# The opening written out up to slot 22, chunk 1 in the geometry of the later chunks, and eight-column softmax pieces on GpSimd

## The chip, the cores and the metric

The kernel runs on one core of a Trainium2 chip. Its time is the device time of one execution in microseconds; lower is better. A core has a matrix engine (TensorE, PE in the rows), a vector engine (VectorE, DVE), an activation engine (ScalarE, ACT), GpSimd (POOL) and a queue engine that issues most transfers (SyncE, SP). Each engine takes its instructions strictly in the order of its own program and waits on the others by semaphores.

## What is computed

Windowed attention over 8 batches, 8 heads, 576 tokens and 64 features per head (heads 0 to 3 with a plain window of 32 keys, heads 4 to 7 with a window of 32 keys at a step of 4), and behind it a feed-forward layer over the 4608 tokens with softplus between its two products (512 to 2048 to 512 features).

```
scores = (q @ k.T) / 8, masked to the window
attn   = exp(scores - max) / (sum(exp(scores - max)) + 1e-9)
x      = attn @ v                       # to [4608, 512]
h      = x @ w_in
out    = softplus(h) @ w_out
```

## The kernel before

The tokens are cut into 9 chunks of 512. A chunk's attention is done in 4 groups (pr 0 and 1 with the plain window, 2 and 3 with the stepped one), numbered `4 * chunk + pr`: groups 0 to 3 are chunk 0, 4 to 7 chunk 1, 8 to 11 chunk 2. The feed-forward work of the first three chunks is cut into 48 slots (`RUNS`): slots 0 to 4 are chunk 0 with the blocks 0 to 4 of 128 hidden features, 5 to 14 chunk 1 with blocks 0 to 9, 15 to 25 chunk 0 with blocks 5 to 15, then the rest of chunk 1 and chunk 2. A slot is four `h_part`s (x to hidden, three matmuls each, since every operand is a high and a low part), a softplus, and four `o_part`s (hidden to output, three matmuls each). The weights arrive as 64-bit words, and each of the 32 tiles (`ff`, 0 for w_in and 1 for w_out) is decoded on the chip: a pass on ScalarE, four on VectorE, a copy on ScalarE and a subtraction on VectorE. From slot 22 on, a planner in the program (costs, due times) writes out the order; the change does not touch it.

The order before slot 22 comes from two sources. `OPENING` is a string of words, each of which emits its instructions on the engines they belong to, in the order of the string; it goes up to the `h_part`s of slot 9 and the `o_part`s of slot 7. Behind it, up to slot 21, a loop emits `h_part`s and `o_part`s in turn, with softplus pieces, chunk 2's attention (`attend`, at the times `ATTENDED` and `VALUED`) and what is left of the decoding between them by a running account of VectorE's time. The words, by engine:

- SP: `k q v` load a group's keys, queries, values, `m` a mask, `r` a decoded tile's raw words (two halves of 256 KB each); the first 90 of these loads have at most 6 under way.
- PE: `F`/`f` fillers that read a zeroed tile and whose result nobody reads, `S` scores (64 small matmuls, and 2 that add the mask), `T` four transposes of the weights, `V` 64 small matmuls with the values, `H{slot}_{kt}` and `O{slot}_{m}` one part.
- DVE: `M` maximum (and, in a group of chunks 0 and 1, the scaling of the 8 columns `nm` by 1/8), `Z` divisor (guard of the 8 sums `sm`, then the reciprocal `ri`), `Pv` division of the 512 columns, `Xt` transposes of the result, `Xl` its low part, `G` softplus's last step, `Gl` its low part, `D1 D2 D3 D4` and `Dl` the decoding.
- ACT: `E` eight exponentials, `C` copy of the transposed weights, `Xh` high part of x, `A` abs, exp and log of a slot, `Gs` high part, `D0` and `D5` of the decoding, `K` copy of an output bank that is set aside.

A group runs S, M, E, Z, Pv, T, C, V, Xt, Xh, Xl. `H` of a slot needs `Xl` of the two groups that make its half of x (`H0_0` and `H0_1` groups 0 and 1, `H0_2` and `H0_3` groups 2 and 3), `Dl` of its w_in tile, and for its first part `G` of the slot two before. `O` needs `Gl` of its slot and `Dl` of its w_out tile. Groups of chunk 2 and later are laid out by heads instead (`self.c >= FIRST`): no division and no turn on PE; the weights are turned in squares on VectorE, sent to memory and fetched back, and the result is divided when it is read from PSUM, by eight copies with a scale on ScalarE (`shares`). `PLACES` says for each of the first 8 groups which PSUM banks its scores, its turn and its result use.

Of the kernel before, what the change touches and what calls it, by code (L numbers as in the profile page):

```python
# [109 lines left out]
D2_4_1 C6 O2_2 V6 D3_4_1 Z7 D2_3_1 D3_3_1 Xt6 D4_3_1 D0_5_0 G4 Pv7 O2_3 H6_0 D5_3_1 Xh6 Gs3 Xl6 D4_4_1  # L110
D1_5_0 r15 T7 r16 m2 r17 q8 r18 H6_1 Dl3_1 D2_5_0 Gl3 C7 Gs4 V7 r19 D0_7_0 D5_4_1 O3_0 O3_1 D1_7_0 Xt7
Dl4_1 Xh7 Xl7 Gl4 H5_2 H5_3 D0_6_1 O3_2 H6_2 H6_3 D1_6_1 D3_5_0 D2_6_1 A5 O3_3 O4_0 O4_1 D4_5_0 D5_5_0
G5 O4_2 H7_0 D2_7_0 A6 Dl5_0 D3_7_0 D3_6_1 K0 D0_6_0 Gs5 r20 G6 H7_1 O4_3 D1_6_0 D4_6_1 H7_2 H8_0 H8_1
H8_2 D4_7_0 Gl5 D5_6_1 r21 k8 v8 r22 Gs6 D5_7_0 K1 Dl6_1 D2_6_0 Dl7_0 r23 D0_8_0 K2 D0_5_1 K3 H8_3 H7_3
# [2049 lines left out]
```

## Time and profile before

| | |
|---|---|
| median of 3 runs | 830.92 us (830.21 to 831.73) |
| the profiled execution's own time | 832.8 us |
| its span, first to last instruction | 831.0 us |
| PE busy in the span | 804.5 us (97%) |
| DVE busy | 655.4 us (79%) |
| ACT busy | 607.6 us (73%) |
| POOL busy | 57.6 us (7%) |
| mean granted TensorE clock | 0.993 |

The median is what a change is compared with; the rows are of the profiled execution, which took 1.9 us more than the median. Busy time on PE is modelled at a matmul's end and overlaps the next one, so work is better read from the distance between starts. Source lines are those of the kernel before.

### The profile page before, as it was taken

The page shows a single profiled execution, that of the slowest core. Times are in us where ns is not written, and L with a number is a line of the kernel's source. Part 1 is how long each engine was busy: PE and PEld are TensorE (multiplying, and loading weights), DVE is VectorE, ACT ScalarE, POOL GpSimd, SP SyncE. Part 2 cuts the span into 40 slices and gives each one's busy share as a digit, 9 for nine tenths or more (in the row PEclk, how much of TensorE's full clock was granted, in tenths as well). Part 3 has the DMA queues.
Part 4 walks back from the last instruction along what each step waited for, and adds up shares of the span by engine and source line. Part 5 has one row for each costly group of instructions (what it writes and reads, how often), then busy time and mean ns, then how long its engine had stood idle before and what let it go on. Part 6 is the DMA issues. An engine that isn't in the chain of part 4 may idle for free. (4 is left out here: it accounts for less than half of the span.)

```text
span 831.0 us, 19932 instructions
## 1 busy us (share of the span) xinstructions
PE 804.5 (97%) x7861; PEld 648.8 (78%) x7861; DVE 655.4 (79%) x966; ACT 607.6 (73%) x1436; POOL 57.6 (7%) x70
## 2 busy tenths in 40 slices
PE   6789999999999999999999999999999999999997
PEld 3566887887888877778788888878878888888886
DVE  6788889887778779868779988777789877567964
ACT  6677789868787787698899836878887436776732
POOL 0000000030334423000000000000000000000000
PEclk9799999999999999999999999999999999999999
DMA  8973953455999989757787967988877576666662
GB/s 296 320 224 130 307 185 122 134 188 177 330 307 330 311 310 337 265 196 217 225 274 245 322 226 261 290 292 286 243 228 235 167 245 222 190 203 210 219 199 82
DMA packets 105806, 198.35 MB, mean 239 GB/s; under 512 B 9584, under 2 KB 52592, under 8 KB 105712
## 3 DMA queue, kind: packets, MB, share of 16 engines
q1 hardware_dynamic: 105568, 196.78, 71.9%
q8 instruction: 62, 1.02, 0.5%
q10 hardware_dynamic: 144, 0.29, 0.1%
q14 instruction: 32, 0.26, 0.1%
HBM read 148.80 MB, written 48.23 MB: 237 GB/s over the span
## 5 line engine op out<-in xcount | busy, mean ns | idle before, releaser
L246 PE MATMUL o_ps<-g,t 128*128 128x512 f32 x867 | 208.7, 389 | 0.0
L246 PEld LDWEIGHTS o_ps<-g,t 128*128 128x128 f32 x867 | 162.0, 188 | 33.9
L246 PE MATMUL o_ps<-g,parts 128*128 128x512 f32 x576 | 144.1, 393 | 2.1 <-ACT s L488 1.6
L246 PE MATMUL h_ps<-xh,parts 128*128 128x512 f32 x384 | 131.5, 400 | 5.0 <-DVE e L757 2.2
L246 PEld LDWEIGHTS o_ps<-g,parts 128*128 128x128 f32 x576 | 106.7, 188 | 26.7 <-ACT s L488 2.5
L1574 ACT CAST g<-stored 128x1024 fp32r<-128x1024 f32 x72 | 75.6, 1051 | 61.8 <-PE o_ps L246 58.2
L1578 DVE TENSOR_TENSOR g<-stored,g 128x1024 fp32r<-128x1024 f32 x72 | 87.8, 1220 | 27.5 <-ACT g L1574 27.3
L246 PEld LDWEIGHTS h_ps<-xh,parts 128*128 128x128 f32 x384 | 72.8, 190 | 23.6 <-ACT xh L676 3.1
L488 ACT ACTIVATE s<-s,nm 128x64 f32<-128x64 f32 x224 | 75.3, 355 | 4.7 <-DVE nm L477 3.8
L246 PE MATMUL h_ps<-xl,parts 128*128 128x512 f32 x192 | 75.9, 396 | 0.9 <-DVE xl L680 0.9
L894 POOL TENSOR_TENSOR a<-a 128x256 f32<-128x256 f32 x64 | 56.6, 892 | 258.6 <-DVE a L889 239.6
L246 PE MATMUL h_y<-s,t 128*128 128x512 f32 x276 | 70.6, 391 | 0.0
L246 PE MATMUL h_x<-s,t 128*128 128x512 f32 x276 | 70.5, 391 | 0.0
L246 PEld LDWEIGHTS h_x<-s,t 128*128 128x128 f32 x276 | 51.6, 188 | 11.1 <-issue 0.2
L246 PEld LDWEIGHTS h_y<-s,t 128*128 128x128 f32 x276 | 51.5, 188 | 11.0
L1554 DVE SCALAR_TENSOR_TENSOR stored<-stored,e 128x1024 f32<-128x1024 f32 x48 | 58.2, 1216 | 2.2 <-ACT e L1550 2.1
L1569 DVE TENSOR_TENSOR stored<-stored 128x1024 f32<-128x1024 f32 x48 | 58.1, 1214 | 0.2
L623 ACT ACTIVATE pt<-sv_ps,ri 128x64 f32<-128x64 f32 x224 | 48.7, 331 | 10.4 <-DVE s L465 7.7
L1544 ACT ACTIVATE e<-stored 128x1024 f32<-128x1024 f32 x48 | 50.6, 1056 | 3.0 <-DVE stored L1533 2.3
L1550 ACT ACTIVATE e<-e 128x1024 f32<-128x1024 f32 x48 | 50.7, 1060 | 1.0
L1547 ACT ACTIVATE e<-e 128x1024 f32<-128x1024 f32 x48 | 50.7, 1057 | 0.7
L757 DVE SCALAR_TENSOR_TENSOR e<-h_ps,e 128x512 f32<-128x512 f32 x48 | 32.8, 684 | 18.5 <-ACT e L1249 12.3
(107 smaller groups left out, 1250.2 us busy)
## 6 DMA issues: line engine op xcount, KB each, us to landing
t<-w_o SPq DMA_DIRECT2D x84, 512.0 KB, 4.3
raw<-w SPq DMA_DIRECT2D x64, 256.0 KB, 5.2
v<-vp SPq DMA_DIRECT2D x28, 512.0 KB, 5.5
t<-w SPq DMA_DIRECT2D x20, 512.0 KB, 4.1
t<-w_two SPq DMA_DIRECT2D x20, 512.0 KB, 4.6
q<-qp SPq DMA_DIRECT2D x35, 256.0 KB, 4.5
k<-kl SPq DMA_DIRECT2D x28, 320.0 KB, 4.7
w_o<-stage SPq DMA_DIRECT2D x32, 256.0 KB, 4.7
```

Of the source, the lines that this page charges most:

```text
L246: return tc.keep_in_program_order(nc.tensor.matmul(**kw))
L488: pin(nc.scalar.activation(out=self.blocks[:, t], in_=src, func=AF.Exp, bias=self.nm[:, t : t + 1], scale=1.0 / 8.0 if self.masked else 1. ...
L623: divided = nc.scalar.activation(out=self.x[:, n], in_=self.values_in[h][:, at_col : at_col + D], func=AF.Copy, scale=self.ri[:, n : n + 1],)
L757: pin(nc.vector.scalar_tensor_tensor(out=e, in0=tiles.pop(i), scalar=0.0, in1=e, op0=ALU.max, op1=ALU.add))
L894: pin(nc.gpsimd.tensor_tensor(out=out, in0=in0, in1=in1, op=ALU.subtract))
L1544: pin(nc.scalar.activation(out=es[key], in_=raw_g(*key), func=AF.Abs))
L1547: pin(nc.scalar.activation(out=es[key], in_=es[key], func=AF.Exp, scale=-1.0))
L1550: pin(nc.scalar.activation(out=es[key], in_=es[key], func=AF.Ln, bias=1.0))
L1554: pin(nc.vector.scalar_tensor_tensor(out=h, in0=h, scalar=0.0, in1=es.pop(key), op0=ALU.max, op1=ALU.add))
L1569: pin(nc.vector.tensor_tensor(out=raw_g(c, *PLACE[name]), in0=raw_g(c, *PLACE[a]), in1=raw_g(c, *PLACE[b]), op=op))
L1574: pin(nc.scalar.copy(out=set_of(k)[0], in_=raw_g(c, *PLACE[name])))
L1578: pin(nc.vector.tensor_tensor(out=low, in0=raw_g(c, *PLACE[name]), in1=high.bitcast(F32), op=ALU.subtract))
```

## The change

The string `OPENING` now goes up to the end of slot 21's `h_part`s and slot 19's `o_part`s, and the loop, `attend`, `tick`, `decoding` and the events are gone. The new words `U X Y W` are a chunk-2 group's turn, send, fetch and shares; `N` is the second maximum of such a group, and `K4` to `K7` the second set of output banks that is set aside. Thirteen large fillers become one (`F1_0`), behind the first `h_part`. Chunk 1 (groups 4 to 7) takes the layout by heads (`BY_HEAD = 1`) for its keys, queries, values and masks, with its turn still on PE; its `Pv` is gone and it has `W`, the eight scaled copies, in its place; its mask is added from 32 rows through a second constant, `spread`. The scaling of `nm` is taken out of `M` and becomes a word: `Np` runs it on GpSimd (groups 1 to 7), `N` on VectorE (group 0). The guard of `sm` can be taken out of `Z`: `Ep` runs it on GpSimd (all groups but group 0). `PLACES` changes. The instructions that the planner writes from slot 22 on are the same.

```diff
-OPENED = 9
-PLACES = "aoa hoa ooo aoa hoa oaa oaa aaa".split()
+PLACES = "hoa oaa oao aoa haa ooa oaa aaa".split()
+BY_HEAD = 1
-ATTENDED = 10.2, 12.9, 15.6, 19.0
-VALUED = 14.6, 17.1, 19.8
 OPENING = """
-F1 F6 f21 F4 r0 m0 F2 k0 q0 D0_0_0 r1 D0_1_0 D1_0_0 S0 k1 q1 D2_0_0 D3_0_0 D4_0_0 D5_0_0 M0 D1_1_0
-D2_1_0 S1 q3 k3 Dl0_0 E0 M1 D3_1_0 D4_1_0 k2 Z0 q2 S3 S2 k4 E1 M3 D5_1_0 q4 Pv0 T0 M2 E3 Z1 Pv1 Z3 r2 m1
-v0 S4 Dl1_0 M4 v1 C0 k5 q5 r3 E2 T1 V0 C1 D0_0_1 Pv3 Z2 Pv2 T2 Xt0 D1_0_1 Xh0 v2 Xl0 V1 E4 Xt1 Xh1 C2
-D2_0_1 Xl1 D3_0_1 D0_2_0 v3 r4 S5 M5 D4_0_1 Z4 H1_0 E5 r5 D1_2_0 D2_2_0 D3_2_0 k6 q6 H0_0 Pv4 T3 H1_1 r6
-v4 C3 D5_0_1 V2 Xt2 Xh2 T4 Z5 Xl2 C4 V3 r7 Xt3 Xh3 D4_2_0 k7 v5 Pv5 H0_1 D0_1_1 Xl3 D5_2_0 D1_1_1 H1_2
-H1_3 D0_3_0 Dl0_1 A1 Dl2_0 H0_2 H0_3 S6 D1_3_0 D2_3_0 A0 D3_3_0 T5 C5 G1 H2_0 D2_1_1 D3_1_1 D4_3_0
-D5_3_0 H2_1 G0 H2_2 H2_3 M6 Dl3_0 Gs1 Gs0 Gl0 V4 H3_0 H3_1 H3_2 D0_4_0 D0_2_1 D1_2_1 D2_2_1 Xt4 Xh4
-D4_1_1 Xl4 H3_3 O0_0 E6 Gl1 Z6 D5_1_1 D3_2_1 D4_2_1 Dl1_1 D1_4_0 D2_4_0 A2 O0_1 O0_2 G2 V5 Xt5 Xh5
...
-O7_1 r29 r30 Gs8 Dl8_0 Dl5_1 G9 O7_2 Gl8 Dl6_0 O7_3 Gs9 r31 Gl9
+q1 k1 m0 S1 M1 q0 k0 S0 M0 N0 r0 r1 D0_0_0 D1_0_0 D2_0_0 D3_0_0 f21 Np1 E1 Ep1 Z1 D0_1_0 D1_1_0 D2_1_0
+D3_1_0 q3 k3 S3 M3 E0 Pv1 q2 Np3 E3 Ep3 k2 S2 Z0 Pv0 T0 C0 q4 q5 m1 v0 k4 r2 r3 V0 D4_0_0 D5_0_0 M2 Np2 E2
+Ep2 D4_1_0 D5_1_0 Z3 Pv3 Xt0 Xh0 D0_0_1 Dl0_0 S4 M4 Dl1_0 D0_2_0 T1 C1 Z2 Pv2 D1_0_1 D2_0_1 Np4 E4 Ep4
+D1_2_0 Xl0 v1 V1 Xt1 Xh1 k5 D2_2_0 D3_2_0 S5 M5 Np5 Xl1 r4 v3 v2 r5 r6 q6 T2 D0_1_1 D3_0_1 D1_1_1 T3 C3 C2
+H0_0 D2_1_1 E5 Ep5 F1_0 D4_2_0 D5_2_0 V3 Xt3 Xh3 V2 Xt2 Xl3 D4_0_1 D0_3_0 Xh2 Xl2 D1_3_0 Z4 D0_2_1 D1_2_1 Z5
+T5 C5 H1_0 H0_1 T4 C4 D2_3_0 Dl2_0 D3_3_0 D4_3_0 D5_0_1 Dl0_1 H0_2 H0_3 A0 D3_1_1 G0 H1_1 H1_2 H1_3 A1 G1
+D2_2_1 D5_3_0 Dl3_0 r7 k6 v4 v5 r8 q7 r9 r10 r11 S6 M6 Np6 V4 W4 D0_4_0 Gs0 Gs1 Xt4 Xh4 D4_1_1 Xl4 Gl0
+D1_4_0 Gl1 D2_4_0 D3_2_1 D3_4_0 D4_4_0 D0_4_1 D5_1_1 Dl1_1 E6 Ep6 V5 W5 Xt5 H2_0 H2_1 H2_2 H3_0 H2_3 O0_0
+D1_4_1 O0_1 H3_1 H3_2 H3_3 k7 S7 r12 r13 r14 O1_0 O1_1 O0_2 O0_3 M7 Np7 A2 G2 D4_2_1 O1_2 O1_3 D5_4_0 Dl4_0
+A3 G3 Xh5 D2_4_1 Xl5 H4_0 H4_1 H4_2 H4_3 D3_4_1 D5_2_1 D0_3_1 Gs2 Gl2 D1_3_1 Dl2_1 O2_0 D2_3_1 D3_3_1 r15 E7
+D4_4_1 Z6 D0_5_0 T6 H5_0 H5_1 D1_5_0 D0_6_1 v6 C6 V6 Ep7 Z7 O2_1 D1_6_1 D2_6_1 D4_3_1 A4 W6 Gs3 O2_2 O2_3 k8
+v7 r16 r17 G4 D3_6_1 D4_6_1 Gl3 Xt6 T7 D0_5_1 D5_4_1 D1_5_1 D2_5_1 H6_0 H6_1 C7 V7 D5_3_1 Dl3_1 O3_0 O3_1
+O3_2 O3_3 Xh6 Xl6 Gs4 W7 Gl4 Dl4_1 O4_0 O4_1 Xt7 Xh7 D2_5_0 D5_6_1 D0_7_0 D0_6_0 Xl7 H5_2 D3_5_0 D1_7_0
+D3_5_1 D1_6_0 D4_5_1 D2_7_0 H5_3 A5 H6_2 H6_3 A6 m2 r18 q8 D4_5_0 D2_6_0 O4_2 r19 r20 K2 S8 G5 O4_3 G6
+D3_7_0 D4_7_0 D3_6_0 Dl6_1 H7_0 H7_1 H8_0 H8_1 H7_2 H8_2 H7_3 H8_3 Gs5 K3 Gl5 K0 O5_0 D5_7_0 D5_5_1 Dl5_1
+D4_6_0 Gs6 Gl6 O6_0 Dl7_0 D5_5_0 Dl5_0 k9 M8 K1 O5_1 O5_2 D5_6_0 A7 G7 D0_8_0 D1_8_0 N8 D0_7_1 D0_8_1 D1_7_1
+D2_7_1 O5_3 Gs7 Gl7 D1_8_1 D3_7_1 D0_9_0 D1_9_0 A8 G8 O6_1 O6_2 H9_0 H9_1 H9_2 O6_3 H9_3 A9 Gs8 O7_0 H10_0
+O7_1 O7_2 D2_9_0 D2_8_0 D3_8_0 D4_8_0 Dl6_0 D4_7_1 G9 D2_8_1 D3_8_1 E8 D5_7_1 O7_3 Gs9 H10_1 H10_2 Gl8 H11_0
+H11_1 H10_3 O8_0 H11_2 H11_3 D5_8_0 D4_8_1 D3_9_0 Gl9 Dl7_1 U8 A10 G10 Dl8_0 D4_9_0 A11 D0_10_0 q9 r21 r22
+S9 m3 r23 r24 r25 r26 r27 r28 D1_10_0 D2_10_0 Ep8 r29 D0_9_1 D1_9_1 D5_8_1 D5_9_0 Z8 G11 D2_9_1 Dl8_1 D3_9_1
+O8_1 O8_2 O8_3 Gs10 O9_0 O9_1 Gl10 D0_10_1 D1_10_1 M9 O9_2 O9_3 H12_0 H13_0 H12_1 H12_2 Gs11 Gl11 Dl9_0
+D3_10_0 q10 H12_3 D0_12_0 A12 O10_0 O11_0 O10_1 O10_2 D0_11_0 D4_10_0 D5_10_0 D4_9_1 D5_9_1 N9 G12 D2_10_1
+Dl10_0 O10_3 Gs12 Gl12 D3_10_1 D4_10_1 D1_12_0 D2_12_0 X8 Y8 k10 v8 V8 W8 Xt8 E9 U9 Dl9_1 D1_11_0 O11_1
+H13_1 H13_2 H13_3 A13 D2_11_0 G13 H14_0 D5_10_1 D3_12_0 D3_11_0 D4_12_0 Dl10_1 S10 O11_2 H14_1 H14_2 H14_3
+O11_3 D0_13_0 Gs13 Gl13 D0_11_1 A14 G14 X9 m4 M10 N10 H15_0 H15_1 O12_0 H15_2 H15_3 A15 O13_0 O12_1 O12_2
...
+O18_2 O18_3 H21_3 Ep11 Gs20 Gl20 A21 Dl15_1 Z11 X11 Y11 O19_0 O19_1 O19_2 O19_3
 """
-            self.n, self.scaled_by, self.beside = c * NPR + pr, None, None
-            self.own, self.masked = c == 0, c < 2
+            self.n, self.scaled_by, self.beside, self.guarded = c * NPR + pr, None, None, False
+            self.own, self.masked, self.by_head = c == 0, c < 2, c >= BY_HEAD
             self.places = PLACES[self.n] if self.n < len(PLACES) else "aaa"
 
-            if self.c >= FIRST:
-                src = kl[self.c - FIRST, self.pr]
+            if self.by_head:
+                src = kl[self.c - BY_HEAD, self.pr]
-                        col = t * WKEYS
-                        if self.c >= FIRST:
-                            q0, k0, col = g * PER + t * BLK, g * (PER + WIN) + t * BLK, col + t // 2 * MW
+                        if self.by_head:
+                            q0, k0 = g * PER + t * BLK, g * (PER + WIN) + t * BLK
+                        col = t * WKEYS + (t // 2 * MW if self.c >= FIRST else 0)
             if self.masked:
                 for r in range(2):
+                    if self.by_head:
+                        quad = slice(self.pr * SQ, (self.pr + 1) * SQ)
+                        matmul(
+                            out=self.banks[r][:, :SW], lhsT=spread[quad],
+                            rhs=masks[self.c][quad, r * SW : (r + 1) * SW], start=False, stop=True,
+                        )
+                        continue
-                pin(nc.vector.tensor_scalar(
-                    out=nm, in0=nm, scalar1=1.0 / 8.0, scalar2=1.0, op0=ALU.mult, op1=ALU.mult
-                ))
                 return
+        def smaller(self, engine):
+            if engine is nc.scalar:
+                pin(engine.activation(out=self.nm, in_=self.nm, func=AF.Copy, scale=1.0 / 8.0))
+                return
+            pin(engine.tensor_scalar(
+                out=self.nm, in0=self.nm, scalar1=1.0 / 8.0, scalar2=1.0, op0=ALU.mult, op1=ALU.mult
+            ))
+
         def greatest(self):
+            if self.masked:
+                self.smaller(nc.vector)
+                return
+        def guard(self, engine):
+            self.guarded = True
+            pin(engine.tensor_scalar(
+                out=self.sm, in0=self.sm, scalar1=1.0e-9, scalar2=1.0, op0=ALU.add, op1=ALU.mult
+            ))
+
         def divisor(self):
-            sm = self.sm
-            self.ri = ri = wk.tile([P, NB], F32, name="ri")
-            pin(nc.vector.tensor_scalar(
-                out=sm, in0=sm, scalar1=1.0e-9, scalar2=1.0, op0=ALU.add, op1=ALU.mult
-            ))
-            pin(nc.vector.reciprocal(out=ri, in_=sm))
+            self.ri = wk.tile([P, NB], F32, name="ri")
+            if not self.guarded:
+                self.guard(nc.vector)
+            pin(nc.vector.reciprocal(out=self.ri, in_=self.sm))
-            if self.c >= FIRST:
+            if self.by_head:
-            self.x = self.pt.rearrange("p g n -> p (g n)").rearrange("p (b n) -> p b n", n=D)
+            pt = self.pt.rearrange("p g n -> p (g n)") if self.c >= FIRST else self.pt
+            self.x = pt.rearrange("p (b n) -> p b n", n=D)
-            if self.c >= FIRST:
+            if self.by_head:
                 by_square = self.x.rearrange("p b (d k) -> p b d k", d=2)
-                x = x_half(self.c, self.dil)
+                x, j = x_half(self.c, self.dil) if self.c >= FIRST else None, self.j
+                if x is None:
+                    x, j = self.s.rearrange("p (d n) -> p d n", d=2), 0
+                    self.x = x
...
+    shared = {}
+
+    def score_of(n):
+        shared[n] = two_banks("sv_ps")
+        groups[n].score(shared[n])
+
+    def value_of(n):
+
+        m = partner(n)
+        if m < len(groups):
+            groups[n].weighted(shared.pop(m), groups[m])
+        else:
+            groups[n].weighted(two_banks("sv_ps"))
+
     parts = {
...
-        "F": fillers,
+        "F": lambda n, *_: fillers(n),
-        "m": load_mask,
+        "m": lambda n: load_mask(min(n, FIRST), max(n - FIRST, 0)),
-        "S": lambda g: groups[g].score(),
+        "S": lambda g: score_of(g) if g >= FIRST * NPR else groups[g].score(),
+        "N": lambda g: groups[g].greatest(),
+        "Na": lambda g: groups[g].smaller(nc.scalar),
+        "Np": lambda g: groups[g].smaller(nc.gpsimd),
+        "Ep": lambda g: groups[g].guard(nc.gpsimd),
...
-        "V": lambda g: groups[g].weighted(),
+        "V": lambda g: value_of(g) if g >= FIRST * NPR else groups[g].weighted(),
+        "U": lambda g: groups[g].turn_squares(),
+        "X": lambda g: groups[g].send_squares(),
+        "Y": lambda g: groups[g].fetch_squares(),
+        "W": lambda g: groups[g].shares(),
```

## Rows read from the trace of the kernel before

**Rows 1.** Us, busy PE, PEld, DVE, ACT, POOL, clock, DMA share, GB/s by stretch.

```profile
0.00:38.75 38.75, 26.56 (x719) 16.53 (x719) 25.68 (x64) 25.71 (x116) 1.02 (x6) 0.87 0.90 307
38.75:74.24 35.49, 31.61 (x497) 22.94 (x497) 30.17 (x62) 27.11 (x71) 0.00 (x0) 1.00 0.70 232
74.24:172.03 97.79, 97.10 (x842) 78.34 (x843) 85.83 (x163) 81.68 (x204) 0.00 (x0) 1.00 0.51 169
172.03:831.00 658.97, 649.28 (x5804) 531.03 (x5802) 513.76 (x680) 473.10 (x1047) 56.61 (x64) 1.00 0.75 245
```

**Rows 2.** VectorE's timeline: start us, duration us, line, operation.

```profile
38.06 0.69 DVE L680 TENSOR_TENSOR xl<-s,xh 128x512 fp32r<-128x512 f32 x1
...
73.55 0.69 DVE L769 TENSOR_TENSOR g<-e,g 128x512 fp32r<-128x512 f32 x1
```

**Rows 3.** TensorE's timeline.

```profile
73.38 0.73 PE L246 MATMUL o_ps<-g,parts 128*128 128x512 f32 x2
...
139.07 2.88 PE L246 MATMUL o_ps<-g,parts 128*128 128x512 f32 x12
...
172.03 0.39 PE L246 MATMUL h_ps<-xh,parts 128*128 128x512 f32 x1
```

**Rows 4.** VectorE's waits, 38.75 to 74.24: us in total, times, longest.

```profile
DVE sm L500 <- ACT s L488: 1.9, 1, 1.9
```

**Rows 5.** VectorE's timeline at 16 and at 86 us, back to back.

```profile
15.90 0.76 DVE L456 TENSOR_REDUCE nm<-s_ps 128x4 f32<-128x256 f32 x2
16.69 0.17 DVE L461 TENSOR_SCALAR nm<-nm 128x8 f32<-128x8 f32 x1
16.77 0.17 DVE L500 TENSOR_SCALAR sm<-sm 128x8 f32<-128x8 f32 x1
16.97 0.20 DVE L503 RECIPROCAL ri<-sm 128x8 f32<-128x8 f32 x1
17.20 0.69 DVE L506 TENSOR_TENSOR s<-s,ri 128x512 f32<-128x512 f32 x1
...
86.25 0.42 DVE L220 TENSOR_SCALAR a<-a 128x512 int32<-128x512 int32 x1
86.58 0.68 DVE L240 TENSOR_TENSOR parts<-a,parts 128x512 fp32r<-128x512 f32 x1
87.19 0.68 DVE L225 SCALAR_TENSOR_TENSOR a<-raw,a 128x512 int32<-128x512 int32 x1
```

**Rows 6.** ScalarE's timeline.

```profile
8.78 0.66 ACT L214 ACTIVATE a<-raw 128x512 f32<-128x512 f32 x1 [2.52 <-DMA raw<-w]
9.34 0.61 ACT L237 CAST parts<-a 128x512 fp32r<-128x512 f32 x1
9.85 0.32 ACT L488 ACTIVATE s<-s_ps,nm 128x64 f32<-128x64 f32 x1
...
12.51 0.31 ACT L488 ACTIVATE s<-s_ps,nm 128x64 f32<-128x64 f32 x1 [0.18 <-DVE nm L461]
...
78.15 0.60 ACT L750 ACTIVATE e<-h_ps 128x512 f32<-128x512 f32 x1 [1.74 <-PE h_ps L246]
...
129.39 1.73 ACT L623 ACTIVATE pt<-sv_ps,ri 128x64 f32<-128x64 f32 x8
```

**Rows 7.** DMA from 0 to 30 us.

```profile
DMA packets 4810, 8.87 MB, mean 296 GB/s; under 512 B 528, under 2 KB 784, under 8 KB 4805
```

**Rows 8.** Columns of rows 1, for one microsecond.

```profile
24.00:25.00 1.00, 0.00 (x0) 0.00 (x0) 0.14 (x1) 1.00 (x9) 0.00 (x0) 0.50 1.00 361
```

**Rows 9.** GpSimd's groups: count, busy us, mean ns, idle before.

```profile
L894 POOL TENSOR_TENSOR a<-a 128x256 f32<-128x256 f32 x64 | 56.6, 892 | 258.6 <-DVE a L889 239.6 <-DVE parts L916 13.3 <-DVE sm L500 3.2
...
L297 POOL CAST ident<-consts 128x128 f32<-128x128 bf16 x1 | 0.3, 290 | 4.7 <-DMA consts<-cst 4.7
```

**Rows 10.** VectorE's groups, 200 to 300 us, where GpSimd works.

```profile
L889 DVE TENSOR_TENSOR a<-parts 128x512 f32<-128x512 f32 x22 | 16.2, 757 | 0.0
...
L769 DVE TENSOR_TENSOR g<-e,g 128x512 fp32r<-128x512 f32 x16 | 10.9, 682 | 4.9 <-ACT g L763 4.6
```

More of the change, by code (lines that the diff above doesn't have):

```diff
@@ L110 @@
[L110 to L114, printed above, removed]
@@ L709, in values @@
         load_v(n + 1)
-    events, serial = [], itertools.count()
-    def at(when, part, *what, cost=0.0):
-        heapq.heappush(events, (when, next(serial), cost, part, what))
-    def send(n):
-        groups[n].send_squares()
-    def bring(n):
-        groups[n].fetch_squares()
-    def pump(now):
-        spent = 0.0
-        while events and events[0][0] <= now:
-            _, _, cost, part, what = heapq.heappop(events)
-            part(*what)
-            spent += cost
-        return spent
-    STEPS = 2 * NKT
     tiles, ready = {}, {}
@@ L800, in o_part @@
         if final and i < HANDED:
[L801 to L806 removed]
+            keeping[m] = c, o_ps[m]
     def kept_part(m, c, src):
@@ L814, in resumed_part @@
         load_dma(out=out[m * P : (m + 1) * P, c * CH : (c + 1) * CH], in_=obs[m])
-    def softplus_tile(i):
-        activated(i)
-        if i < HANDED - 1:
-            at(i + 1.0, softplus, i, cost=0.69)
-            at(i + 1.125, g_high, i)
-            at(i + 1.375, g_low, i, cost=0.69)
     def fillers(n):
@@ L866, in tile_windowed_attention_softplus_ffn @@
         name = word[:3] if word[0] == "D" and word[1] != "l" else word.rstrip("0123456789_")
-        parts[name](*(int(x) for x in word[len(name) :].split("_")))
+        parts[name](*map(int, word[len(name) :].split("_")))
     fetch(len(needed))
@@ L1066, in decoding @@
-    def decoding(keys):
-        def part(*steps):
-            for key, step in steps:
-                if key < len(keys):
-                    decode_step(*keys[key], step)
-        parts = []
-        for j in range(len(keys) + 1):
-            if j < len(keys):
-                begun = [(0, 0), (1, 0)] if j == 0 else []
-                parts.append((0.84, (*begun, (j, 1), (j, 2))))
-                parts.append((0.69, ((j, 3),)))
-            if j:
-                parts.append((0.69, ((j - 1, 6),)))
-            if j < len(keys):
-                parts.append((0.69, ((j, 4), (j, 5), (j + 2, 0))))
-        return [(0, cost, lambda what=what: part(*what)) for cost, what in parts]
@@ L1086, in tile_windowed_attention_softplus_ffn @@
-    chores = decoding([(ff, i) for _, ff, i in needed if (ff, i) not in words])
-    for j, (when, valued) in enumerate(itertools.zip_longest(ATTENDED, VALUED)):
-        attend(FIRST * NPR + j, when, valued)
-    behind = 0.0
-    def tick(time):
-        nonlocal behind
-        now[0] = time
-        behind += pump(time) - 0.69
-        while chores and behind + chores[0][1] < 0.4:
-            _, cost, chore = chores.pop(0)
-            chore()
-            behind += cost
-        behind = max(behind, 0.0)
@@ L1103, in tile_windowed_attention_softplus_ffn @@
-    for i in range(OPENED + 1, HANDED):
-        for kt in range(NKT):
-            h_part(i, kt)
-            if kt == NKT - 1:
-                softplus_tile(i)
-            tick(i + (kt + 1) / STEPS)
-        for m in range(NKT):
-            o_part(i - LAG, m)
-            tick(i + (NKT + m + 1) / STEPS)
-    pump(HANDED + 0.4)
-    for _, _, chore in chores:
-        chore()
-    assert not events
     MM, LATENCY, RATE, LANDING = 0.227, 0.06, 0.32, 2.3
@@ L2099, in _layout @@
     ], axis=1)
-    qp[FIRST:] = ql[FIRST:].reshape(qp[FIRST:].shape)
-    kl = np.empty((NCH - FIRST, 2, 2, 2, D, 4, per + WIN), np.float32)
-    late = np.empty((NCH - FIRST, 2, 2, 2, WKEYS, 2, 2, 4, D), np.float32)
-    for c in range(FIRST, NCH):
+    qp[BY_HEAD:] = ql[BY_HEAD:].reshape(qp[BY_HEAD:].shape)
+    kl = np.empty((NCH - BY_HEAD, 2, 2, 2, D, 4, per + WIN), np.float32)
+    late = np.empty((NCH - BY_HEAD, 2, 2, 2, WKEYS, 2, 2, 4, D), np.float32)
+    for c in range(BY_HEAD, NCH):
         for j in range(2):
@@ L2140 @@
     masks = _masks()
-    arrays["msk"] = _late_masks(masks).astype(ml_dtypes.bfloat16)
+    late = _late_masks(masks)[FIRST - BY_HEAD :]
+    arrays["msk"] = late.reshape(NCH - FIRST, NPR, P, 2 * SW).astype(ml_dtypes.bfloat16)
     eye = np.eye(P, dtype=ml_dtypes.bfloat16)
     arrays["cst"] = np.stack(
-        [np.concatenate([eye, (8.0 * m).astype(ml_dtypes.bfloat16)], axis=1) for m in masks[:2]]
+        [
+            np.concatenate([eye, np.tile(eye[:BLK, :BLK], (NG, NG)), (8.0 * m).astype(ml_dtypes.bfloat16)], axis=1)
+            for m in (masks[0], _late_masks(masks)[0, :, 0].reshape(P, 2 * SW))
+        ]
     )
```

100 lines of the change are left out of this document (30 added, 70 removed).

## The prediction, made before the change had run

> **What bounds the kernel now.** I read first the busy times cut at three points of the program [rows 1]: the end of the last low part of chunk 0's x (`Xl3`, the VectorE row that starts at 38.06 and takes 0.69), the end of what slot 3's first output part needs (`Gl3`, starting at 73.55) [rows 2], and the first `h_part` of slot 22, at 172.03 [rows 3]. The reader is to see two regimes. From 74 us on TensorE has 97.10 of 97.79 us busy, and after 172 us 649.28 of 658.97: there only less TensorE work would save time. Ahead of 74 us TensorE has gaps (31.61 of 35.49, and 26.56 of 38.75, fillers included), and VectorE is nearly full. Then I read what VectorE waits for between 38.75 and 74.24 [rows 4]: the largest wait, 1.9, is for a group's exponentials, that is, for the group's own chain.
>
> **The accounts.** The words of either string say how many passes each engine has ahead of a point, and the distance from start to start what a pass costs. VectorE [rows 5]: a maximum 0.79, the scaling of `nm` 0.08, the guard 0.20, the reciprocal 0.23, a 512-column pass 0.61, one that reads a single float tile (`D1`, `D2`) 0.33; an `Xt` I put at a long pass, 0.68. ScalarE [rows 6]: `D0` 0.56, a copy or cast 0.51, a group's eight exponentials 2.5 (the next group's start, less its 0.18 of idle), a slot's abs, exp and log 1.8 (three of 0.60), the eight scaled copies of a `W` 1.73.
>
> **TensorE's work** is the same in both: ahead of `O3_0` either list has 24 parts of `H`, 12 of `O` and 8 each of `S`, `T` and `V`, only in another order. From there to slot 22 the same matmuls remain. So the question is when `O3_0` can begin, and whether TensorE stays full behind it.
>
> **Stage 1, to the end of chunk 0's x.** VectorE before: 6 maxima, 6 scalings, 8 short and 10 long passes of the decoding, 6 whole `Z` (0.43), 6 `Pv`, 4 `Xt`, 4 `Xl`: 25.1 us, in 38.75, so 13.6 us are start and waiting. After, ahead of `Xl2`: 6 maxima, 1 scaling, 10 short and 10 long passes, one whole `Z` and three bare reciprocals, 4 `Pv` (chunk 1's two are gone), 4 `Xt`, 4 `Xl`: 22.8 us. With the same 13.6 of waiting it ends at 36.4; with 0.2 more for each of five GpSimd hops on the way, at 37.4, the upper bound. The lower bound is the loads. Up to `v2`, the last one needed, the new list loads 8,320 KB, 8.52 million bytes, and the first 30 us of before moved 8.87 million [rows 7], so `v2` lands about 28.8; `V2`, `Xt2`, `Xh2`, `Xl2` take some 0.9, 0.7, 0.6 and 0.7 behind it: 31.7. Between the two I walked the three lists with these costs: scores of group 1 at about 7, its exponentials from 9.5 (behind `D0_0_0`, whose raw words stand as far down the list, 1.8 million bytes, as those of the pass that began at 8.78 did before [rows 6]), E0 to 14.8, E3 to 17.5, E2 to 21, C1 to 23.7, V1 to 24.9, E4 to 26.0, Xl1 to 28.1, E5 to 30.6, V2 to 31.9, Xl2 to 34.4. I take 35.2, 0.8 more for what such a walk leaves out.
>
> The fillers cost nothing to remove where TensorE waits for loads, but they were also work on it. In before the clock stood at its upper level up to 23 us, and in the microsecond at 24, without a matmul in it, at 0.50 (1.2 of 2.4 GHz) [rows 8]. After the change the small blocks of `S`, `T` and `V` probably run at 1.2 GHz from the start; the walk costs them so.
>
> **Stage 2, from there to `O3_0`.** VectorE before: 14 short and 19 long passes of the decoding, 9 of softplus, 2 maxima with scalings, 2 whole `Z`, 2 `Pv`, 3 `Xt`, 3 `Xl`: 29.2 us, in 35.49, 6.3 over. ScalarE before: 7 `D0`, 15 copies, 5 slots, 2 groups' exponentials: 25.6. After, VectorE: 15 short, 21 long, 9 of softplus, 2 maxima, 4 bare reciprocals, 3 `Xt`, 2 `Xl`: 28.8. ScalarE: 7 `D0`, 17 copies, 5 slots, 2 exponentials and three `W`: 3.9 + 8.7 + 9.0 + 5.0 + 5.2 = 31.8. So the `W`s, which replace four divisions of 0.61 on VectorE by four times 1.73 on ScalarE, make ScalarE the longer one. Lower bound 31.8, upper 31.8 + 6.3 = 38.1. I take 34.2, under half of that surplus, because the wait of before [rows 4] sits in the chain E, Z, Pv, T, and in chunk 1 `T` now follows E directly.
>
> **Stage 3, from `O3_0` to slot 22.** The same matmuls: 97.8 (97.1 with the 0.7 of idle gone). VectorE has 85.83 busy there and ScalarE 81.68 [rows 1]; either keeps some 12 us of cover, which is what hides the rest of the edits: `K`, `W`, `U` and `Xt` of chunk 2 are the ones that the loop issued, and the raw loads end later (`r31` beside slot 14) but are asked for in the order of use. On SP `k10` and `v8` now stand behind `X8 Y8`, a trip to memory and back, and `V8` is the next word on TensorE that needs them: the first place where a wait could show.
>
> **The sum.** 35.2 + 34.2 + 97.8 = 167.2 instead of 172.0: 4.8 less. What follows slot 22 is the planner's list, untouched: 659.0. The span of 831.0 becomes 826.2, the execution's own 832.8 becomes 828.0, and, as that execution lies 1.9 above the median of the runs shown, the median 830.92 becomes 826.1. Bounds together: 31.7 + 31.8 + 97.1 = 160.6, 11.4 less; 37.4 + 38.1 + 97.8 = 173.3, 1.3 more.
>
> **GpSimd's pieces.** The trace has no pass of 8 columns on GpSimd. Its nearest rows are a cast of 128 columns, 0.29, and a two-input pass of 256 columns, 0.89 [rows 9]. VectorE's own was 0.08 from start to start, so a piece in the chain M, Np, E costs between 0.2 and 0.8 more. I take 0.3, near the cast; the walk has it. Behind an `Np` on ScalarE the whole list waits, copies and decoding too. `Ep` is covered: the `Z` behind it stands after other VectorE words. What speaks against: beside GpSimd's passes a two-input VectorE pass takes 0.757, away from them 0.682 [rows 10]. The Trainium skill (SBUF — State Buffer, Who interferes with whom) says that VectorE instructions with two SBUF inputs and GpSimd instructions that read SBUF lock each other out for a whole instruction. The two rows agree in direction only. By that rule, as an estimate, each of seven pieces could wait for one VectorE pass, and the sum would come near 831.
>
> **The rivals.**
> *More is gained*: stage 1 near its bound of loads and stage 2 near ScalarE's sum, 33 + 32 + 97.5 = 162.5, 9.5 less: 821.4. For it: both lists leave much room. Against: no stage ahead of 74 us has come near its sum before [rows 1].
> *ScalarE eats it*: stage 2 keeps 6.3 on top of ScalarE's 31.8, and stage 1 its 13.6: 36.4 + 38.1 + 97.8 = 172.3, no change, 831.2.
> *The written order starves TensorE later* (the slower side): where the order was a written string, in stage 2, TensorE stood 3.9 of 35.5 us, 11%; in stage 3, most of it written by the loop, 0.7 of 97.8. The stretch that is newly written, from slot 10 on, is some 72 us. At 11% it costs 7.9, and the kernel is slower by 3.1: 834.0. It decides from 4.8 us, 7%, on. Against it: the 12 us that VectorE and ScalarE have to spare there.
> *GpSimd holds the chain*: at 0.8 more for each of the seven `Np`, 5.6, against 2.1 in my sum: 3.5 later, 829.6; if each waits for a VectorE pass of 0.68 too, 4.8 more: 834.4.
> *The clock*: TensorE stays at 1.2 GHz until the `H` parts of slots 0 and 1 are done. Twelve matmuls in a row take 2.88 at the upper level [rows 3], 0.23 each; eight parts of three at double that are 5.5 us later, of which the ScalarE work beside them hides over half: 2.3 later, 828.4.
>
> **How the numbers follow.** A measurement tells 0.2%, 1.7 us, from no change. My forecast (823 to 829) has 0.45, more gained 0.14, the clock 0.08, ScalarE 0.11, the written order 0.13, GpSimd 0.09. Faster: 0.45 + 0.14 + 0.08 + 0.02 of the last two = 0.69; no change: 0.11 + 0.05 of these two = 0.16; slower: the other 0.15 of them. The time is that of the forecast, 826.1. The range is 821.0 to 832.5: it leaves out the very end of the gain and the slower ends of the last two.
>
> **What would show it.** Right: chunk 0's x complete near 35 instead of 38.75, `O3_0` near 69 instead of 73.4, slot 22 near 167, ScalarE busier than VectorE between the first two, and the same 659 behind slot 22. Wrong: TensorE idle by several us between 75 and 167; exponentials that wait for GpSimd; a half clock beyond 40 us; or another distance from slot 22 to the end.

## The result, and the profile after

The changed kernel takes 822.87 us (median of 4 runs, 822.52 to 823.02), the kernel before 831.33 beside it (830.21 to 831.97): a ratio of 0.990, interval 0.988 to 0.992, 8.4 us less. The prediction said 826.1, 4.8 less than the median it was made against. The profiled execution took 822.52 with a span of 820.7; that of before 832.8 and 831.0, so between the two traces there are 10.3 us to place.

The busy times after, by stretch (columns as in [rows 1]), cut at the end of chunk 0's x, at the first matmul of `O3_0` and at slot 22:

```profile
0.00:35.06 35.06, 22.85 (x708) 16.76 (x708) 23.14 (x53) 26.02 (x117) 4.40 (x16) 0.76 0.90 303
35.06:68.73 33.67, 31.37 (x496) 24.43 (x495) 28.49 (x59) 30.96 (x94) 1.17 (x4) 0.95 0.93 310
68.73:166.25 97.52, 97.52 (x850) 78.71 (x845) 87.56 (x164) 84.55 (x215) 1.55 (x4) 1.00 0.48 153
166.25:820.70 654.45, 648.32 (x5804) 530.72 (x5802) 508.90 (x672) 473.24 (x1044) 56.82 (x64) 1.00 0.76 248
```

The cuts come from these rows of the timelines after: VectorE, where `Xl2` is now the last low part of chunk 0's x [rows 2], and TensorE [rows 3].

```profile
34.37 0.69 DVE L718 TENSOR_TENSOR xl<-s,xh 128x512 fp32r<-128x512 f32 x1
```

```profile
68.73 4.62 PE L261 MATMUL o_ps<-g,parts 128*128 128x512 f32 x18
...
166.25 0.39 PE L261 MATMUL h_ps<-xh,parts 128*128 128x512 f32 x1
```

The marks lie at 38.75, 73.38 and 172.03 before [rows 1, 3] (the second stretch of [rows 1] ends 0.9 later, at 74.24). So 5.8 us are gained ahead of slot 22 (3.7 to the first mark, 1.0 to the second, 1.1 to the third), and 4.5 behind it, where the instructions are the same. From 68.73 to slot 22 TensorE has not one gap.

The stretch from 35 to 68.7 has one wait on TensorE (line of the waits; then its timeline, and ScalarE's `W4`):

```profile
PE a_ps L261 <- ACT pt L658: 2.3, 1, 2.3
```

```profile
42.75 1.35 PE L261 MATMUL a_ps<-v,pt 64*32 64x64 f32 x64 [2.28 <-ACT pt L658]
```

```profile
40.96 1.74 ACT L658 ACTIVATE pt<-a_ps,ri 128x64 f32<-128x64 f32 x8
```

It is `V5`, which writes the bank that `W4` reads, and `W4` stands behind two slots' softplus passes on ScalarE.

Behind slot 22, TensorE's waits before:

```profile
PE sv_ps L246 <- issue: 1.4, 1, 1.4
PE h_ps L246 <- DVE e L757: 1.2, 1, 1.2
PE h_y L246 <- issue: 1.0, 1, 1.0
PE h_x L246 <- DVE e L757: 0.8, 1, 0.8
PE sv_ps L246 <- PE h_y L246: 0.5, 1, 0.5
PE sv_ps L246 <- DMA pt<-turned: 0.4, 1, 0.4
...
```

and after:

```profile
PE h_ps L261 <- DVE e L773: 1.1, 1, 1.1
PE h_x L261 <- DVE e L773: 0.8, 1, 0.8
...
```

Two stops in which the profile shows nothing to wait for ("issue", 1.4 and 1.0, at 557 and 401 us) and a late fetch of turned weights near 607 (0.4 and 0.5) are gone: 3.3 us. Matmul for matmul, the distance between the two traces grows by 0.4 near 188 us, 1.1 at 401, 1.6 at 557 and 1.2 near 607, so 3.9 of the 4.5 lie at these three places. The 0.4 is a leftover of the order ahead of slot 22: a weight load of the kernel before waits for a low part.

```profile
188.07 1.00 PEld L246 LDWEIGHTS o_ps<-g,parts 128*128 128x128 f32 x5 [0.51 <-DVE g L769]
```

What makes the stops, the first four experiments ask.

### The profile page after: what moved, and what is told of

Read it like the earlier page. It is cut to its first block, busy times and chain, and to the rows that moved or that the text cites. A ratio compares the mean times of both kernels' runs of the same rounds, so it can differ in the third digit from the quotient of the medians.

```text
span 820.7 us, 19960 instructions
## 1 busy us (share of the span) xinstructions
PE 800.1 (97%) x7849; PEld 650.6 (79%) x7849; DVE 648.1 (79%) x945; ACT 614.8 (75%) x1468; POOL 63.9 (8%) x88
## 4 chain that ended last, share of the span: by engine, by line
PE 94%; ACT 2%; DVE 2%; DMA 0%; issue 0%; POOL 0%; SPq 0%; DVEq 0%; ACTq 0%; POOLq 0%
PE o_ps L261 44%; PE h_ps L261 16%; PE h_y L261 14%; PE h_x L261 14%; PE sv_ps L261 5%; ACT s L518 1%; PE s_ps L261 1%; PE a_ps L261 1%; DMA k<-kpl 0%; PE t_ps L551 0%; DVE a L381 0%; ACT pt L658 0%; DVE s L381 0%; ACT pt L589 0%; DVE nm L478 0%
## 5 line engine op out<-in xcount | busy, mean ns | idle before, releaser
L1502 DVE TENSOR_TENSOR g<-stored,g 128x1024 fp32r<-128x1024 f32 x72 | 87.8, 1221 | 26.1 <-ACT g L1498 25.9
L773 DVE SCALAR_TENSOR_TENSOR e<-h_ps,e 128x512 f32<-128x512 f32 x48 | 32.9, 686 | 23.0 <-ACT e L1173 17.3
```

The source lines that it names most:

```text
L773: pin(nc.vector.scalar_tensor_tensor(out=e, in0=tiles.pop(i), scalar=0.0, in1=e, op0=ALU.max, op1=ALU.add))
L1502: pin(nc.vector.tensor_tensor(out=low, in0=raw_g(c, *PLACE[name]), in1=high.bitcast(F32), op=ALU.subtract))
```

## The experiments

All ratios are to the kernel before, on the same chip, with 95% intervals. A time at slot 22 or behind it is that of one profiled execution.

**What is gained behind slot 22.** Both kernels once more, and the fillers taken out of the one and put into the other:

```diff
-F1 F6 f21 F4 r0 m0 F2 k0 q0 D0_0_0 ...
+r0 m0 k0 q0 D0_0_0 ...
```

```diff
-q1 k1 m0 S1 M1 q0 ...
+F1 F6 f21 F4 F2 q1 k1 m0 S1 M1 q0 ...
```

> The kernel before, unchanged, profiled a second time. In its first profile TensorE stood 1.0, 1.4 and about 1.1 us behind slot 22 (at 402, 557 and 611 us) and 4.8 us ahead of 27 us with nothing that the profile shows to wait for. Theory P (the place in the program makes these stops): the same stops at the same places, and again about 659 us from slot 22 to the end. Theory R (each execution has its own): stops elsewhere or none, slot 22 within 2 us of 172, and 655 to 658 us behind it.

> The changed kernel, unchanged, profiled a second time and timed beside the others. Theory P (the stops of TensorE behind slot 22 hang on where its instructions lie): slot 22 begins within 1 us of 166.25 and again about 654.5 us follow it. Theory R (each execution has its own stops): another distance, 654 to 659.

> The kernel before without its fillers (34 matmuls that nobody reads), everything else alike. In both its profiles it stopped behind slot 22 at the same places (at 401, 557 and 611 us, 3.1 and 3.7 us together). Theory P (these stops hang on where the instructions of TensorE lie, and any other count of them ahead moves them): other stops or none there, and up to 3.7 us less behind slot 22. Theory Q (they hang on the transfers of that time, which the fillers do not touch): the same stops. For the opening: theory A (the fillers hold the clock up): slot 22 begins 1 to 4 us later than 172; theory B (they only cover a wait for loads): at 171 to 173.

> The changed kernel with the first fillers of the kernel before (34 matmuls that nobody reads) back at the head of the list. Theory P (stops behind slot 22 hang on the number of instructions ahead of them on TensorE): stops there again, more than 655.5 us behind slot 22, and the time 1 to 3 us up by these alone. Theory Q (they hang on the transfers of that time): 654 to 655 again. In the opening, theory A (the fillers delay the scores or hold the clock): slot 22 moved by over 1 us; theory B (ScalarE's exponentials set the pace there): 165.5 to 167.

The kernel before again: slot 22 at 171.60 and 658.36 behind it, with stops of 1.2 and 0.7 at the two places of the first profile, as theory P has it. The changed kernel again: ratio 0.991 (0.989 to 0.993), slot 22 at 167.17, 655.23 behind it, no such stop, but 0.4 for the late fetch, which therefore comes and goes by the execution. Two executions of one kernel differ by 0.4 and 0.9 at slot 22, and by 0.6 and 0.8 behind it. Before without fillers: 0.998 (0.997 to 0.999), slot 22 at 171.05 (theory B) and 656.59 behind it; the two old places are free, and one stop, of 0.6, stands at 592. So a change of nothing but the number of matmuls ahead took 1.8 to 2.4 us off an untouched stretch.

With the fillers in the changed kernel: 0.995 (0.993 to 0.997), 2.8 to 3.7 us later at slot 22 (169.95) and 655.55 behind it. Theory P expected stops there, and there are none: the 0.3 to 1.1 more than without fillers are about what the late fetch makes (0.8 here, none and 0.4 there). The stop came in the opening instead. It is on TensorE's timeline of that kernel, in the middle of the four transposes of one `T`:

```profile
...
32.85 0.33 PE L551 MATMUL t_ps<-ident,s 128*128 128x128 f32 x1
35.35 0.55 PE L551 MATMUL t_ps<-ident,s 128*128 128x128 f32 x3 [2.17 <-issue]
...
```

Chunk 0's x was complete at 35.49 (35.06 and 36.57 without fillers); the stop, and half clock in the matmuls behind it (0.50 granted from 36.5 to 39.9), are the loss. A stop between two transposes that need nothing new can't be a wait for data. The page of the profile after has a queue of kind instruction (queue, packets, MB, share; first row), and in the kernel with fillers one packet of it lies between 32.9 and 34.0 (second row):

```profile
...
q8 instruction: 62, 1.02, 0.5%
...
```

```profile
...
q8 instruction: 1, 0.02, 5.4%
...
```

62 packets of 16 KB stand against 2 times 7849 rows of TensorE, matmuls and weight loads: 253 to a packet. Set side by side, from the trace's rows (matmuls counted from the program's start; us):

```
kernel           matmuls ahead   block landed   TensorE goes on
before                347            17.50           18.81
before                473            24.10           25.56
before again          347            18.41           19.93
before again          473            24.00           25.41
before, no fillers    221            15.13           16.57
before, no fillers    473            25.24           26.87
after, fillers        727            33.89           35.35
V5 late               854            40.54           41.85
before               4669           399.58          400.80
before               6307           555.75          557.06
```

Neighbouring stops stand 126 or 127 matmuls apart (347 and 473, 727 and 854) and the others at about a multiple of that, whatever instruction is there, and each ends 1.2 to 1.6 us after an instruction block landed. So TensorE stands until its next block of instructions is there. Seven of these ten blocks took 0.9 to 1.1 us to move, like most of the 62: what was late was mostly the start of the transfer, and why it was late was not tried.

Theory P holds in part. The place in the program decides where a stop can be. The two kernels with the old order (below), whose TensorE list is that of before, stop at the place of 401 us again, though they reach it 10 us later (first row: the one without pieces). But the place alone does not decide whether a stop is there. The kernel with the pieces on VectorE (below) has the TensorE list of the changed kernel, and stops 1.2 us (second row) at a block that came late in neither profile of the changed kernel.

```profile
410.71 0.98 PE L261 MATMUL h_y<-a,parts 128*128 128x512 f32 x3 [1.00 <-issue]
```

```profile
559.33 0.85 PE L261 MATMUL h_y<-s,t 128*128 128x512 f32 x3 [1.19 <-issue]
```

The Trainium skill (Runtime: NRT & Kernel Launch, Instruction fetch mechanics) says that the sequencer streams its instructions in blocks of 16 KiB, 256 of them, and that crossing into the next is mostly hidden. The size agrees with the 62 packets. "Mostly" holds by count: in the first profiles five of the 62 blocks came late in the kernel before, and one in the changed kernel. A late one cost 0.2 to 2.2 us.

**What is gained ahead of slot 22: the parts or the order.** The order of before, word for word, with the new parts (and once without the pieces), and the new order with chunk 1's old layout:

```diff
-PLACES = "hoa oaa oao aoa haa ooa oaa aaa".split()
+PLACES = "aoa hoa ooo aoa hoa oaa oaa aaa".split()
-q1 k1 m0 S1 M1 q0 k0 S0 M0 N0 r0 r1 ...
+F1 F6 f21 F4 r0 m0 F2 k0 q0 D0_0_0 r1 ...
...
-... S6 M6 Np6 V4 W4 D0_4_0 ...
+... M6 Np6 Dl3_0 Gs1 Gs0 Gl0 V4 W4 H3_0 ...
```

```diff
-BY_HEAD = 1
+BY_HEAD = 2
-... Z4 D0_2_1 D1_2_1 Z5
+... Z4 Pv4 D0_2_1 D1_2_1 Z5 Pv5
-... V4 W4 D0_4_0 ...
+... V4 D0_4_0 ...
...
-            for m in (masks[0], _late_masks(masks)[0, :, 0].reshape(P, 2 * SW))
+            for m in (masks[0], masks[1])
```

> The order of the kernel before, written out word for word up to slot 22 (what its loop issued too, and its fillers and its choice of banks), with the changed kernel's geometry of chunk 1 and its pieces on GpSimd: W directly behind V, Np directly behind M, Ep directly behind E. Theory A (the new order makes the gain, the parts alone nothing): near the kernel before, 829 to 833. Theory B (geometry and pieces make the gain by what they take off VectorE): near the changed kernel, 823 to 826.

> The order of the kernel before, written out word for word, with the changed kernel's geometry of chunk 1 (W directly behind V) and nothing on GpSimd: the scaling behind the maximum, the guard inside Z. With geometry and pieces together that order began slot 22 at 181.7, against 172.0 of the kernel before. Theory A (the geometry costs it: W's 1.73 us on ScalarE stand in the chain and in the way of the softplus): 179 to 182, and the time within 3 us of that of both together. Theory B (the pieces cost it: a hop for every maximum in the chain): 172 to 175, near the kernel before.

> The changed kernel with chunk 1 in the layout of chunk 0 again: four divisions of 0.61 on VectorE (directly behind their reciprocals) instead of four times eight scaled copies of 1.73 on ScalarE. Theory A (ScalarE is the longer engine between chunk 0's x and O3_0, as the prediction took it, and the one gap of 2.3 us on TensorE there, V5 waiting for W4, comes from it): 2 to 4 us faster than the changed kernel, 819 to 821. Theory B (the division in front of the turn lengthens the chain and fills VectorE where it has least room): 1 to 5 us slower, 824 to 828.

Old order, new parts: 1.014 (1.012 to 1.017), slot 22 at 181.66, 9.6 later than before. Without the pieces nearly the same: 1.012 (1.011 to 1.014), 181.94. In that trace TensorE's list is that of before, VectorE's lacks chunk 1's four divisions and ScalarE's has the four `W` more, so the layout, with `W` directly behind `V`, is what costs it (theory A of that run). The stretches 2 and 3 of the kernel without pieces (columns as above), and TensorE's waits in its stretch 2:

```profile
38.39:80.01 41.62, 34.26 (x496) 24.87 (x496) 29.10 (x60) 31.59 (x94) 0.00 (x0) 0.89 0.63 207
80.01:181.94 101.93, 99.73 (x850) 80.05 (x845) 86.18 (x163) 84.61 (x214) 0.00 (x0) 0.98 0.47 161
```

```profile
PE o_ps L261 <- ACT s L518: 3.6, 1, 3.6
PE h_ps L261 <- DVE e L773: 2.9, 1, 2.9
...
```

ScalarE has 31.59 of work there, as in the changed kernel (30.96), but in the old order it holds up others: an `O` part waits 3.6 us for the bank that a group's exponentials still read (1.6 in the kernel before), an `H` part 2.9 for a softplus (1.1). New order, old layout: 1.003 (1.001 to 1.004), slot 22 at 177.36. Here `T` waits for the division on VectorE:

```profile
PE t_ps L551 <- DVE s L540: 6.4, 2, 5.1
PE a_ps L261 <- issue: 3.2, 1, 3.2
...
```

(The 3.2 stands on no instruction block; there `V5` writes the bank that VectorE's `Xt4` still reads.) For the old order with all parts both theories fell; for the old layout theory B had the direction, with some 10 us where it said 1 to 5. Neither the order alone nor the parts alone gain anything; together they gain 5.8. Which part of the new order does it (the words, the loads, the banks of `PLACES`) was not taken apart.

**The pieces on GpSimd.**

```diff
-        "Np": lambda g: groups[g].smaller(nc.gpsimd),
+        "Np": lambda g: groups[g].smaller(nc.vector),
-        "Ep": lambda g: groups[g].guard(nc.gpsimd),
+        "Ep": lambda g: groups[g].guard(nc.vector),
```

The other two take out all words `Ep` (the guard falls back into `Z`), or all `Np` and write `M1 N1` for `M1`, and so on.

> The changed kernel with all its eight-column pieces (7 scalings, 11 guards) on VectorE again, at the same places of the order. Theory A (a piece on GpSimd costs the chain about 0.3 us more, as the prediction took it, and seven of them are in the chain): 1 to 2 us faster than the changed kernel, 821 to 822. Theory B (the hop is hidden, and what counts is that VectorE is rid of some 0.1 to 0.2 us per piece and of waiting in line for the sums): 1 to 3 us slower, 824 to 826. Neither matters: within 0.5 us of 822.9.

> The changed kernel with the eleven guards inside Z again, on VectorE directly in front of the reciprocal; only the seven scalings stay on GpSimd. With the guards on VectorE at their early places the kernel lost 12.8 us of VectorE to waits for exponentials. Theory A (that loss is the waiting in line, not the pass: a guard taken where its reciprocal stands costs its 0.2 us and no wait): within 1.5 us of the changed kernel, a ratio of 0.988 to 0.992 to the kernel before. Theory B (the order leans on the guards being off VectorE): over 3 us slower than the changed kernel, above 0.994.

> The changed kernel with the seven scalings of nm on VectorE directly behind the last pass of their maximum; the guards stay on GpSimd. Theory A (a hop to GpSimd and back costs the chain from maximum to exponentials about 0.3 us more than VectorE's 0.08, as the prediction took it, and the chain bounds): 1 to 2 us faster than the changed kernel, a ratio of 0.987 to 0.989. Theory B (the hop is hidden): no difference, 0.9895 to 0.9905. Theory C (the order leans on it): slower, above 0.992.

Both on VectorE at the same places: 1.003 (1.001 to 1.004), slot 22 at 175.27, 9.0 later than in the changed kernel. VectorE's waits up to 50 us, and one of them on its timeline:

```profile
DVE sm L529 <- ACT s L518: 12.8, 5, 3.3
...
```

```profile
26.32 0.17 DVE L529 TENSOR_SCALAR sm<-sm 128x8 f32<-128x8 f32 x1 [3.31 <-ACT s L518]
26.40 0.68 DVE L245 SCALAR_TENSOR_TENSOR a<-raw,a 128x512 int32<-128x512 int32 x1
```

A pass of 0.17 holds up VectorE's whole list for 3.31 us, decoding included, because its word stands where GpSimd could wait at leisure. Theory B had the direction, with some 10 us where it said 1 to 3. With the guard where its reciprocal is, nothing is lost: 0.990 (0.988 to 0.992), slot 22 at 165.24. Nor with the scaling behind its maximum: 0.991 (0.989 to 0.992), 166.79. So either kind of piece, well placed, is worth nothing that can be measured on GpSimd or on VectorE, and taking out the hop from maximum to exponentials gained nothing. Both kinds off GpSimd at once, each well placed, were tried in the old order alone, with 1.012 against 1.014.

**What bounds the opening.**

```diff
-... Ep6 V5 W5 Xt5 H2_0 H2_1 H2_2 H3_0 ...
+... Ep6 H2_0 H2_1 H2_2 V5 W5 Xt5 H3_0 ...
```

```diff
-... N0 r0 r1 D0_0_0 D1_0_0 D2_0_0 D3_0_0 f21 Np1 E1 Ep1 Z1 D0_1_0 D1_1_0 D2_1_0 D3_1_0 q3 k3 S3 M3 E0 ...
+... N0 r0 r1 f21 Np1 E1 Ep1 D0_0_0 D1_0_0 D2_0_0 D3_0_0 Z1 D0_1_0 q3 k3 S3 M3 Np3 E0 D1_1_0 D2_1_0 D3_1_0 ...
```

> The changed kernel with V5 (and W5, Xt5) moved behind H2_0 H2_1 H2_2. In the changed kernel TensorE stands 2.3 us in front of V5, until W4 has read the bank, and its clock is at half from 43.5 to 46.5 behind that, some 1.5 us more; those three parts could run in the gap, and nobody needs V5 before 48. Theory A (from 35 us on TensorE is the bound, so a gap closed there is gained whole): 2 to 4 us faster than the changed kernel, a ratio of 0.985 to 0.988 to the kernel before. Theory B (VectorE's and ScalarE's sums set when the softplus and the low parts come, as the prediction's account of this stretch has it): the wait shows up again before O3_0, and less than 1 us is gained, 0.989 to 0.991.

> The kernel with V5 late, and with the first exponentials moved up: E1 ahead of D0_0_0 on ScalarE (which stands there until 8.5 us for raw words, with the maximum of group 1 done at 7.6), and M3 and Np3 ahead of the second pass of decoding on VectorE. In the changed kernel ScalarE is busy 23.2 of the 25 us from 10 to 35. Theory A (ScalarE bounds the stretch up to chunk 0's x, and what it starts earlier is gained): chunk 0's x complete near 34 instead of 35.1, slot 22 at 162.7 to 163.5, 0.5 to 1.3 us before that of the kernel with V5 late. Theory B (the last values to land, or VectorE, bound it): 164 again, or later.

`V5` late: 821.20 us, 0.988 (0.987 to 0.990). Its marks on TensorE's timeline, and stretch 2:

```profile
66.50 4.65 PE L261 MATMUL o_ps<-g,parts 128*128 128x512 f32 x18
...
163.98 0.39 PE L261 MATMUL h_ps<-xh,parts 128*128 128x512 f32 x1
```

```profile
35.01:66.50 31.49, 30.49 (x496) 22.97 (x495) 28.57 (x59) 30.53 (x94) 0.92 (x4) 1.00 0.92 309
```

The 2.3 us are gained whole, up to slot 22 (163.98 against 166.25), but not the 1.5 more for the clock: a stop at an instruction block, up to 41.85, and a wait for a bank, up to 47.08, took it back (0.5 and 0.4 of idle time, 0.7 each from start to start). By the ratios it is 1.4 to 2.3 us faster than the changed kernel, with intervals that overlap.

Ahead of that, chunk 0's x was complete at 35.06 in the changed kernel and at 35.01 with `V5` late. The clock of the stretch from 13 to 29.5 (column before the last two; first the changed kernel, then `V5` late) seems to differ:

```profile
13.00:29.50 16.50, 12.98 (x346) 9.37 (x346) 15.27 (x36) 14.81 (x73) 2.79 (x7) 0.50 0.95 316
```

```profile
13.00:29.50 16.50, 12.84 (x414) 9.02 (x408) 14.85 (x34) 14.38 (x70) 2.94 (x7) 1.00 0.95 321
```

But the 1.00 does not fit the second kernel's own rows. A group's 64 small score matmuls took 0.86 at the upper level (first row, the changed kernel at 52 us), and 1.19 and 1.17 in the two kernels at 19.5 us:

```profile
52.34 0.86 PE L261 MATMUL s_ps<-k,q 64*32 64x64 f32 x64
```

```profile
19.44 1.19 PE L261 MATMUL s_ps<-k,q 64*32 64x64 f32 x64
```

```profile
19.52 1.17 PE L261 MATMUL s_ps<-k,q 64*32 64x64 f32 x64
```

So both ran at the pace of the lower level there (1.2 of 2.4 GHz), and what the clock is worth up to chunk 0's x is not shown. The early exponentials on top of late `V5`: 0.990 (0.989 to 0.991), slot 22 at 164.73, no gain. `E1` began at 7.87 instead of 8.73, but chunk 0's x was complete at 35.69, no earlier. One wait of TensorE's transposes is new, for a guard (first row); in the kernel with `V5` late `T` waited 0.9 for a division there (second row).

```profile
PE t_ps L551 <- POOL sm L529: 1.4, 1, 1.4
...
```

```profile
...
PE t_ps L551 <- DVE s L540: 0.9, 1, 0.9
```

The rest of the way is not shown. Theory A fell as tried; whether ScalarE bounds that stretch in another order was not tried.

## Why the prediction was right, and where not

The opening came as forecast, with its mechanism; the time itself came 3.2 us lower, 0.1 below the forecast's own band of 823 to 829, because a term behind the opening was taken as fixed.

**Stage 1.** Taken 35.2, measured 35.06, and 36.57 in the second profile. The walk holds in its steps too: exponentials from 9.11 (9.5 in the walk), those of group 4 done at 25.9 (26.0), the last low part at 35.06 (34.4). VectorE's accounts are added up 0.1 to 0.3 too low from the costs given (25.4, 22.9, 29.4 and 29.0 come out for 25.1, 22.8, 29.2 and 28.8), which moves nothing that was taken.

**Stage 2.** Taken 34.2, measured 33.67. The sum of ScalarE, 31.8, is 30.96 busy, and the surplus of 2.4 is not the chain E, Z, T, but one gap of 2.28, `V5` behind `W4`. That `W` on ScalarE is the price of the new layout was right; 31.8 as the lower bound was a little high: with the gap closed the stretch took 31.49, with ScalarE and TensorE both at 30.5.

**Stage 3.** Taken 97.8, measured 97.52 without a gap, so *the written order starves TensorE later* did not happen, and the trip behind which `k10` and `v8` stand on SP held up nothing.

**Slot 22** then came at 166.25 and 167.17, where 167.2 was said.

**Behind slot 22: the step that failed.** "What follows slot 22 is the planner's list, untouched: 659.0." It took 654.45 and 655.23. The list is untouched, but its place in TensorE's instruction stream moved, and with it the stops at instruction blocks; in the first two traces these two places make 2.7 of the 4.5, the late fetch, which also comes and goes without a change, 1.2, and the leftover at 188 us 0.4. The rows already had it: behind 172 us TensorE was busy 649.28 of 658.97 [rows 1], and "only less TensorE work would save time" passed over the 9.7 between. Over the two profiles of each kernel, slot 22 came 4.4 to 5.8 us earlier and 3.1 to 4.5 fell away behind it: the medians are 8.4 apart, the first two traces 10.3. That the stops fell the kernel's way was luck; the kernel with the pieces on VectorE has one of 1.2 back.

**GpSimd's pieces.** The price of 0.3 for each of seven was too high: none of it shows in the time. What the row said [rows 9, 10] is there in the pieces themselves, on GpSimd's timeline (with two of VectorE's passes behind it):

```profile
7.60 0.20 POOL L499 TENSOR_SCALAR nm<-nm 128x8 f32<-128x8 f32 x1 [1.26 <-DVE nm L478]
...
14.56 0.49 POOL L499 TENSOR_SCALAR nm<-nm 128x8 f32<-128x8 f32 x1 [2.70 <-DVE nm L478]
...
26.11 0.66 POOL L529 TENSOR_SCALAR sm<-sm 128x8 f32<-128x8 f32 x1 [3.64 <-ACT s L518]
```

```profile
14.31 0.68 DVE L540 TENSOR_TENSOR s<-s,ri 128x512 f32<-128x512 f32 x1
...
26.02 0.69 DVE L240 SCALAR_TENSOR_TENSOR a<-raw,a 128x512 int32<-128x512 int32 x1
```

A piece takes 0.20 where VectorE stands idle. The other two begin inside a 512-column pass of two inputs and end 0.06 behind it, at 15.05 and 26.77. The Trainium skill (SBUF — State Buffer, Who interferes with whom) gives such a lock, and the trace agrees; [rows 10] alone, two lines of one stretch, could not tell. But up to chunk 0's x ScalarE waited 0.6 us in all for a scaled maximum, so the 831 by that rule did not come, and *GpSimd holds the chain* fell with it. What I had not seen is the other side: where a guard waits early, it holds up VectorE by 12.8 us if it stands there, and on GpSimd hardly anybody (VectorE 1.0 us up to 50 us).

**The rivals.** *ScalarE eats it* is what happens, and more, when the new layout meets the old order: 181.9 at slot 22. *The clock*: half clock in the opening was in the walk, and the walk came out. It was up again from 29.8 on, ahead of all `H` parts but the first, so the rival did not come. But it fell once more behind the gap in front of `V5`, a "half clock beyond 40 us" that the prediction had named as a sign of being wrong; it cost the 1.5 named above:

```profile
43.39:46.80 3.41, 3.41 (x57) 2.66 (x37) 2.70 (x6) 3.41 (x12) 0.00 (x0) 0.50 0.99 281
```

*More is gained*: its 821.4 lies nearer to the measured time than the forecast, but not for its reason; the opening gained 5.8, not 9.5.
